# A long-convolution block and its MLP on one core: taps laid apart, evictions in runs of eight, boundary rows shifted by a product, one load queue with six transfers under way

## The chip, the cores and the metric

The kernel runs on one core of a Trainium2 chip. Its time is the device time of one execution in microseconds (us). Five engines work side by side, each through its own list of instructions in order: PE (TensorE, matrix products), DVE (VectorE), ACT (ScalarE), POOL (GpSimd) and SP (SyncE, which here only issues DMA transfers). An instruction that must wait holds up everything behind it in its engine's list.

## The reference

With S = 2048 rows (time), D = 640 channels and F = 1728, all float32:

```python
mod = silu(c) @ w_mod                       # six rows of D: sa, ca, ga, sb, cb, gb
h  = layernorm(x) * (1 + ca) + sa           # x is A_q
ks = sum_t shift(k, t) * shift_k[:, t]      # causal conv of 4 taps along S, per channel
kv = ks * v
y  = longconv(kv, ssm_k) + kv * ssm_D       # causal, length S, per channel (by FFT)
x  = x + ga * (h * y)
h  = layernorm(x) * (1 + cb) + sb
x  = x + gb * (relu(h @ w1 + b1)**2 @ w2 + b2)
```

## The kernel before, in words

**Two stages.** The first computes the long convolution by a transform of length 4096 written as matrix products, in five blocks of 128 channels (`b` = 0 to 4). The second is the MLP over eight chunks of 256 rows with split-precision weights; it is nearly all PE work and the change does not touch it. The second can begin when the last block of the first is done.

**The first stage, per block.** `load_kv(s, u)` brings k and v for a group `s` (group 0 is block 0, groups 1 and 2 are two blocks each) in units `u`: two units for group 0, four for the others, ten in all. A unit is 128 x 1024 numbers; partition p = 32a + n holds, for channel group a, the 64 time steps of segment n. Each unit's k and v come in four transfers of 32 partitions each (128 KB), into two slots for k and two for v in the tile `KV`. `kv(s, u)` forms the 4-tap convolution: four products of k with a tap (one straight into the two-bank PSUM tile `ps6`, three into tiles `up`), three sums into `ps6`, and a product with v into `px[b]` (tiles `S0p`, `S1p`). For groups 0 and 1 two of the four products run on POOL, for group 2 all on DVE. The taps stand in `tapb` (part of `KV`) as they come from memory, channel by channel with the four taps of a channel side by side, so that one tap is read with a step of four numbers.

The first three rows of a unit's k belong to the unit before it (ACT copies them), or, for unit 0, to the neighbouring partition: there POOL clears the three rows and ACT's queue loads them from memory in eight small transfers per group.

`unit_a(b, i, n)` transforms `px[b]` (i = 0) or the filter `ph[b]` (i = 1, loaded by `load_h`) by 64-wide products into two PSUM banks; ACT evicts each bank into the tile `a` with its axes permuted. `spectra` are the second transform, `front` multiplies the two spectra on DVE and POOL, `back` and `unit_y` transform back, `prep` and `finish` apply the layer norm of x and the gate. Beside all this run the six rows of `mod` (loads `wm`) and the row statistics of x (`q_stats`: loads of q, BN_STATS on DVE).

**What sets the order.** The program is recorded as a graph; a planner lists the nodes with costs per engine and with priorities from the table `URGE`, and each engine's list is written out in the planned order. At run time every list is obeyed as it stands. `sp_issue` adds one more rule: each transfer of SP's queue waits until the one `OUT` places ahead of it has landed. All instructions of the graph carry the line number of the call in `emit` (L402), so they are told apart by tiles.

Of the kernel before, what the change touches and what calls it, by code (L numbers as in the profile page):

```python
# [25 lines left out]
OUT = 4  # L26
# [87 lines left out]
class Graph:  # L114
# [101 lines left out]
    def order(self, lag=0.06, pelag=0.1, phase=0.0):  # L216
# [92 lines left out]
        dma_free, landed = 0.0, []  # L309
# [95 lines left out]
def _constants():  # L405
# [17 lines left out]
    for mm in range(1, 32):  # L423
# [32 lines left out]
        "cw": np.hstack([cw, gb[:, 0, 1, 0], gx]).astype(f),  # L456
# [7 lines left out]
def ssm_mlp_kernel(  # L464
# [37 lines left out]
    ident = sb.tile([P, P], F32, tag="ident", name="ident")  # L502
# [7 lines left out]
    cst = sb.tile([P, 256], F32, tag="cst", name="cst")  # L510
# [3 lines left out]
    ca = cst[:, 192:256]  # L514
    warm = sb.tile([P, 1], F32, tag="warm", name="warm")
    nc.scalar.dma_start(cst[:, 0:192], cw_d[:, 0:192])
# [123 lines left out]
    def cost(engine, op, args, kw):  # L640
# [7 lines left out]
        if engine == "DVE":  # L648
            if op == "bn_stats":
                return 0.15 + 0.001 * n  # L650
            if op in ("tensor_mul", "tensor_add", "tensor_sub") and not deep:
                return 0.1 + 0.00115 * n
            if op == "bn_aggr":
                return 0.21
            return 0.17 + 0.001 * n if op != "scalar_tensor_tensor" else 0.17 + 0.00112 * n
# [168 lines left out]
    def load_gi(i):  # L824
        g.key = ("lgi", 0)
        o = slice(8 * i, 8 * i + 8)
        sp_dma(gi[:, 0, o], gi_d.rearrange("p (g c n) -> p g c n", g=16, c=2)[:, o], 4096)
        g.key = ("gi", 0)
        act.activation(gi[:, 1, o, 0], gi[:, 0, o, 1], AF.Copy, scale=-1.0)
        act.activation(gi[:, 1, o, 1], gi[:, 0, o, 0], AF.Copy)  # L830
        if i == 0:
            g.key = ("lgi", 0)
            sp_dma(gi[0:64, 1, 0].rearrange("p c n -> p (c n)"), cw_d[0:64, 192:320], 512)
# [6 lines left out]
    def load_taps(first):  # L840
        g.key = ("ltap", 0)
        if first:
            src = shift_k[:P].rearrange("(a c) t -> a (c t)", a=4)
            sp_dma(tapb[:, 0:128], src.unsqueeze(1).to_broadcast([4, 32, 128]), 512)
            return
        for s in range(2):
            src = shift_k[P + 256 * s : P + 256 * s + 256].rearrange("(a c) t -> a (c t)", a=4)
            sp_dma(tapb[:, 128 + 256 * s : 384 + 256 * s], src.unsqueeze(1).to_broadcast([4, 32, 256]), 1024)
# [4 lines left out]
    def load_kv(s, u):  # L853
# [20 lines left out]
    def kv(s, u):  # L874
# [3 lines left out]
        taps = tapb[:, at : at + 4 * w].rearrange("p (c t) -> p t c", t=4)  # L878
# [3 lines left out]
        for t in range(4):  # L882
            o = sbuf(f"ktmp_{s}_{u}_{t}", (P, n, w), TMP) if t else acc
# [22 lines left out]
    def unit_a(b, i, n):  # L906
# [139 lines left out]
    def load_xp(s, j):  # L1046
# [211 lines left out]
    def mlp_out(n):  # L1258
# [18 lines left out]
        if n < NC - 1:  # L1277
# [4 lines left out]
        ("b1", 0): [-1209, -1601],  # L1282
        ("comb", 0): [-569, -607, -593, -579, -617, -600, -611, -573, -586, -662, -650, -689, -696, -758, -751, -815,
            -822, -847, -840],
        ("comb", 1): [-1052, -1072, -1065, -1058, -1090, -1076, -1083, -1150, -1130, -1136, -1143, -1179, -1186,
            -1213, -1220, -1256, -1263, -1283, -1290],
        ("comb", 2): [-1544, -1493, -1547, -1504, -1554, -1580, -1523, -1573, -1566, -1669, -1662, -1648, -1655,
            -1759, -1720, -1843, -1850, -1864, -1857],
        ("comb", 3): [-2037, -2022, -2047, -2040, -2061, -2065, -2054, -2107, -2100, -2133, -2126, -2140, -2147,
            -2188, -2181, -2214, -2268, -2247, -2261],  # L1290
        ("comb", 4): [-2398, -2412, -2416, -2423, -2429, -2448, -2441, -2456, -2462, -2469, -2505, -2539, -2532,
# [400 lines left out]
```

## Time and profile before

| | us |
|---|---|
| median of 3 runs | 739.98 (738.59 to 777.24) |
| the profiled execution, its own time | 739.45 |
| its span, first to last instruction | 737.7 |
| PE busy | 646.3 (88% of the span) |
| DVE busy | 452.9 (61%) |
| ACT busy | 337.4 (46%) |
| POOL busy | 268.7 (36%) |

The span is what the views divide; 1.75 us of the execution's time lie around it. Busy shares are averages over both stages, which have different limits, so they have to be read stage by stage. A row of a tile view reads: engine, operation, out<-in, count, then the shortest, median and longest duration in ns.

### The profile page before, as it was taken

How to read it: one execution, taken by the hardware profiler on the slowest of the kernel's cores; microseconds unless marked ns; L12 is line 12 of the kernel's file. 1: busy time of each engine (PE TensorE's matmuls, PEld its weight loads, DVE VectorE, ACT ScalarE, POOL GpSimd, SP SyncE). 2: the span in 40 equal slices, each digit the busy share in tenths (PEclk: the TensorE clock that was granted, in tenths of full speed). 3: DMA queues.
4: the chain of work that ended last, by engine and by line, in shares of the span. 5: the costliest groups of instructions: out<-in, count | busy, mean ns of one | idle time of the engine just before them, and what ended most of it. 6: DMA issues, size and time to landing. Idle time of an engine off the chain costs nothing.

```text
span 737.7 us, 17486 instructions
## 1 busy us (share of the span) xinstructions
PE 646.3 (88%) x7401; PEld 574.6 (78%) x7401; DVE 452.9 (61%) x754; ACT 337.4 (46%) x639; POOL 268.7 (36%) x259
## 2 busy tenths in 40 slices
PE   0048798978698989989999999999999999999996
PEld 0047575867577878849999988999999999999896
DVE  1798789789997736786526437446456365464432
ACT  1157256588768798655423424324324233243220
POOL 4647470666655765843311132102103004021001
PEclk9989999988889999998999999999999999999999
DMA  8698689979607521344201011002010020020011
GB/s 113 121 180 194 160 226 234 240 176 190 151 2 150 166 85 45 111 129 129 68 1 42 32 36 36 1 1 72 1 41 33 1 72 1 1 72 1 1 37 36
DMA packets 108155, 62.47 MB, mean 85 GB/s; under 512 B 78316, under 2 KB 98220, under 8 KB 108076
## 3 DMA queue, kind: packets, MB, share of 16 engines
q1 hardware_dynamic: 101884, 58.02, 33.3%
q10 hardware_dynamic: 5936, 3.32, 2.0%
q8 instruction: 58, 0.95, 0.6%
q14 instruction: 21, 0.17, 0.1%
q0 software_dynamic: 256, 0.00, 0.0%
HBM read 52.15 MB, written 9.18 MB: 83 GB/s over the span
## 4 chain that ended last, share of the span: by engine, by line
PE 74%; DVE 7%; DMA 7%; ACT 6%; issue 3%; POOL 3%; SPq 0%; ACTq 0%; DVEq 0%; POOLq 0%
PE ps L402 74%; ACT a L402 5%; DMA KV<-in_A_k_dram 2%; DVE up L402 2%; DMA KV<-in_A_v_dram 2%; DVE ps L402 1%; POOL up L402 1%; DVE wx L402 1%; DMA wm<-in_w_mod_dram 1%; DVE mtmp L402 1%; DMA gb<-in_gb_dram 1%; DMA S1p<-in_A_ssm_k_dram 1%; POOL wx L402 0%; SPq L617 0%; ACTq L402 0%
## 5 line engine op out<-in xcount | busy, mean ns | idle before, releaser
L402 PE MATMUL ps<-xt,w_S 128*128 128x256 f32 (+1 forms) x680 | 129.3, 331 | 0.0
L402 PEld LDWEIGHTS ps<-xt,w_S 128*128 128x128 f32 x680 | 104.8, 190 | 10.3 <-DVE xfs L402 0.2
L402 ACT ACTIVATE mtmp<-ps,b1t 128x256 f32<-128x256 f32 (+1 forms) x112 | 51.4, 473 | 113.7 <-PE ps L402 108.2
L402 PE MATMUL ps<-a,gb 128*64 128x128 f32 x1260 | 82.0, 281 | 8.7 <-DVE wx L402 5.1
L402 PEld LDWEIGHTS ps<-a,gb 128*64 128x64 f32 x1260 | 71.5, 140 | 22.5 <-DVE wx L402 7.4
L402 ACT ACTIVATE a<-ps 128x512 f32<-128x512 f32 x80 | 77.3, 1105 | 20.0 <-PE ps L402 19.7
L402 DVE TENSOR_TENSOR mtmp<-ps,mtmp 128x256 f32<-128x256 f32 (+1 forms) x99 | 41.1, 419 | 69.0 <-ACT mtmp L402 68.0
L402 PE MATMUL ps<-w_S,hring 128*128 128x320 f32 x456 | 78.0, 310 | 0.0
L402 POOL TENSOR_TENSOR wx<-wx 128x256 f32<-128x256 f32 x80 | 68.1, 872 | 20.0 <-DVE wx L402 19.7
L402 PEld LDWEIGHTS ps<-w_S,hring 128*128 128x128 f32 x456 | 70.1, 188 | 1.4
L402 DVE TENSOR_TENSOR hring<-mtmp,hring 128x256 fp32r<-128x256 f32 x74 | 36.3, 496 | 53.8 <-ACT hring L402 53.8
L402 PE MATMUL ps<-cst,S0p 64*64 64x64 f32 x1024 | 24.6, 255 | 50.3 <-DMA KV<-in_A_k_dram 43.2
L402 PEld LDWEIGHTS ps<-cst,S0p 64*64 64x64 f32 x1024 | 21.9, 165 | 55.4 <-DVE S0p L402 45.7
L402 ACT ACTIVATE hring<-mtmp 128x256 fp32r<-128x256 f32 x74 | 30.6, 416 | 67.9 <-PE ps L402 51.3
L402 POOL TENSOR_TENSOR x<-x,gb2row 128x640 f32<-128x640 f32 x16 | 25.3, 1594 | 90.6 <-ACT mtmp L402 90.6
L402 DVE TENSOR_TENSOR wx<-ps,wx 128x512 f32<-128x512 f32 x64 | 40.9, 685 | 22.8 <-PE ps L402 21.8
L402 POOL TENSOR_TENSOR x<-mtmp,x 128x640 f32<-128x640 f32 (+1 forms) x9 | 13.5, 1506 | 108.0 <-DVE mtmp L402 108.0
L402 POOL TENSOR_TENSOR up<-KV 128x1024 f32<-128x1024 f32 x12 | 38.0, 3188 | 27.7 <-DVE ps L402 16.6
L402 DVE TENSOR_TENSOR up<-KV 128x1024 f32<-128x1024 f32 x18 | 43.0, 2396 | 5.3 <-DMA KV<-in_A_k_dram 4.8
L402 DVE SCALAR_TENSOR_TENSOR mtmp<-mtmp 128x256 f32<-128x256 f32 x91 | 44.9, 500 | 1.8
L402 PE MATMUL ps<-gi,wx 64*128 64x128 f32 x640 | 41.5, 278 | 4.4 <-ACT q L402 2.0
L402 ACT ACTIVATE wx<-ps 128x512 f32<-128x512 f32 x49 | 29.5, 608 | 32.3 <-PE ps L402 29.1
(156 smaller groups left out, 1318.6 us busy)
## 6 DMA issues: line engine op xcount, KB each, us to landing
wm<-in_w_mod_dram SPq DMA_DIRECT2D x25, 320.0 KB, 4.1
KV<-in_A_k_dram SPq DMA_DIRECT2D x40, 128.0 KB, 3.7
KV<-in_A_v_dram SPq DMA_DIRECT2D x40, 128.0 KB, 4.5
S1p<-in_A_ssm_k_dram SPq DMA_DIRECT2D x20, 256.0 KB, 5.3
q<-in_A_q_dram SPq DMA_DIRECT2D x8, 640.0 KB, 4.3
out_dram<-x SPq DMA_DIRECT2D x14, 320.0 KB, 3.6
w1s<-in_B_w_dram SPq DMA_DIRECT2D x13, 320.0 KB, 3.4
w2s<-in_B_w_dram SPq DMA_DIRECT2D x13, 320.0 KB, 2.9
```

The source lines that it names most:

```text
L402: fn(*real, **{k: a.real() if isinstance(a, View) else a for k, a in kw.items()})
```

## The change

It does six things:

1. `load_taps` loads the taps into a staging tile and lets ACT copy them into `tapb` tap by tap, so that a product of k with a tap reads neighbouring numbers. Three ACT copies are new.
2. The evictions of `unit_a` walk the bank in another order: they write runs of eight neighbouring numbers where they wrote pairs 32 numbers apart, and read PSUM with a step of 64 numbers.
3. The three boundary rows of each group's unit 0 come as four transfers of 32 partitions into `XP1c`, one product with a shifted identity (`step`) moves them one partition down, and ACT writes them into the k tile, scaled by 0 for the first partition of each channel group and by 1 elsewhere (`later`). POOL's clearing and the 24 small transfers of ACT's queue go.
4. The loads of x for `prep` that ACT issued go to SP's queue.
5. `OUT` is 6 instead of 4.
6. The planner's costs are altered and the table `URGE` is new, so all lists are new.

```diff
-OUT = 4
+OUT = 6
...
-        dma_free, landed = 0.0, []
+        dma_free, landed = 2.5, []
...
-    ident = sb.tile([P, P], F32, tag="ident", name="ident")
+    step = sb.tile([P, P + 1], F32, tag="ident", name="step")
+    ident, step = step[:, 1:], step[:, 0:P]
+    nc.vector.memset(step[:, 0:1], 0.0)
...
+    later = cst[:, 192:193]
...
         if engine == "DVE":
+            if o.buf.name[:3] == "px_":
+                return 0.2 + 0.0017 * n
...
     def load_taps(first):
-        if first:
-            src = shift_k[:P].rearrange("(a c) t -> a (c t)", a=4)
-            sp_dma(tapb[:, 0:128], src.unsqueeze(1).to_broadcast([4, 32, 128]), 512)
-            return
-        for s in range(2):
...
+        raw = sbuf(f"tap_{int(first)}", (P, D), [whole(f"STG{i}") for i in range(4)])
+        for s in (0,) if first else (1, 2):
+            at, w = (0, 128, 384)[s], WIDE[s]
...
+            copy(
+                act,
+                tapb[:, at : at + 4 * w].rearrange("p (t c) -> p c t", t=4),
+                raw[:, at : at + 4 * w].rearrange("p (c t) -> p c t", t=4),
+            )
...
         if u == 0:
-            pool.memset(kt[:, 0:3], 0.0)
-        else:
-            copy(act, kt[:, 0:3], KT[s, u - 1][:, n : n + 3])
+            end = sbuf(f"kend_{s}", (P, 3, w), [part(parent("XP1", 2560), 2048, ("XP1c",))])
         for a in (0, 2, 1, 3):
...
             if u == 0:
-                act_dma(kt[32 * a + 1 : 32 * a + 17, 0:3], kshift[0:16, 0:3, cols], 4 * w)
-                act_dma(kt[32 * a + 17 : 32 * a + 32, 0:3], kshift[16:31, 0:3, cols], 4 * w)
+                sp_dma(end[32 * a : 32 * a + 32], ksrc[:, 61:64, cols], 4 * w)
...
+        if u == 0:
+            t = psum(f"kend_{s}", (P, 3, w), ANY)
+            with g.as_one(0.3):
+                mm(t.rearrange("p i c -> p (i c)"), step, end.rearrange("p i c -> p (i c)"), True, True)
+            act.activation(kt[:, 0:3], t, AF.Copy, scale=later)
+        else:
+            copy(act, kt[:, 0:3], KT[s, u - 1][:, n : n + 3])
...
-        taps = tapb[:, at : at + 4 * w].rearrange("p (c t) -> p t c", t=4)
+        taps = tapb[:, at : at + 4 * w].rearrange("p (t c) -> p t c", t=4)
...
-            o = AX[b][i].rearrange("p m (e d g) -> p m g e d", e=2, d=2)[:, :, 8 * n : 8 * n + 8, e]
-            copy(act, o, t[e].rearrange("p g m d -> p m g d"))
+            o = AX[b][i].rearrange("p m (e d g) -> p m e d g", e=2, d=2)[:, :, e, :, 8 * n : 8 * n + 8]
+            copy(act, o, t[e].rearrange("p g m d -> p m d g"))
...
-            (act_dma if h else sp_dma)(
-                t[64 * h : 64 * h + 64], qsrc[h, :, 4 * j : 4 * j + 4, BASE[s] : BASE[s] + w], 4 * w
-            )
+            sp_dma(t[64 * h : 64 * h + 64], qsrc[h, :, 4 * j : 4 * j + 4, BASE[s] : BASE[s] + w], 4 * w)
...
-        ("kv", 0): [-140, -127, -153, -153, -178, -202, -227, -239, -255, -267, -280, -226, -292, -177, -304, -316],
...
+        ("pa", 0): [-279, -289, -259, -269, -299, -308, -313, -318, -422, -427, -441, -446, -479, -484, -469, -474],
```

**Place 1: the start of SP's list** (transfers; `gb` is a constant of the second transform, `S1p` the filter of block 0, `XP1p` the staged boundary rows, `tap` the staged taps). Before:

```order
L617 DMA KV<-in_A_shift_k_dram 128x1x256
L617 DMA KV<-in_A_k_dram 32x32x32 x2
L617 DMA KV<-in_A_shift_k_dram 128x1x256
L617 DMA KV<-in_A_v_dram 32x32x32 x2
L617 DMA KV<-in_A_shift_k_dram 128x1x128
L617 DMA KV<-in_A_k_dram 32x32x32 x4
L617 DMA KV<-in_A_v_dram 32x32x32
```

The same place in the changed list:

```order
L621 DMA gb<-in_gb_dram 128x1024
L621 DMA KV<-in_A_k_dram 32x32x32 x3
L621 DMA XP1p<-in_A_k_dram 32x3x32
L621 DMA KV<-in_A_k_dram 32x32x32 x2
L621 DMA XP1p<-in_A_k_dram 32x3x32
L621 DMA KV<-in_A_k_dram 32x32x32 x2
L621 DMA tap_122<-in_A_shift_k_dram 128x1x128
L621 DMA KV<-in_A_v_dram 32x32x32
L621 DMA XP1p<-in_A_k_dram 32x3x32
L621 DMA KV<-in_A_k_dram 32x32x32
L621 DMA S1p<-in_A_ssm_k_dram 32x32x64
```

The constant `gb` and the filter of block 0 have moved ahead of most of v; the four filter transfers end at the 24th transfer of the list (they ended at the 34th), and the last quarter of v for unit 1 of group 0 stands 38th, behind the first two loads of q (it stood 21st).

**Place 2: the start of DVE's list** (`ps` the sum in PSUM, `up` a product, `S0p` the result for block 0; `s<-q` and `st<-s` are statistics of x). Before:

```order
L402 TENSOR_TENSOR up_132<-KV 128x1024
L402 TENSOR_TENSOR ps_96<-KV 128x1024
L402 TENSOR_TENSOR ps_96<-ps_96,up_132 128x1024 x3
L402 TENSOR_TENSOR S0p<-ps_96,KV 128x32x32
L402 TENSOR_TENSOR ps_96<-KV 128x1024
L402 TENSOR_TENSOR up_132<-KV 128x1024
L402 TENSOR_TENSOR ps_96<-ps_96,up_132 128x1024
```

The same place in the changed list:

```order
L402 TENSOR_TENSOR ps_97<-KV 128x1024
L402 TENSOR_TENSOR up_142<-KV 128x1024
L402 TENSOR_TENSOR ps_97<-ps_97,up_142 128x1024 x3
L402 TENSOR_TENSOR S0p<-ps_97,KV 128x32x32
L402 BN_STATS s_200<-q_148 128x6
L402 TENSOR_TENSOR up_142<-KV 128x1024
L402 TENSOR_TENSOR ps_97<-KV 128x1024
L402 TENSOR_TENSOR ps_97<-ps_97,up_142 128x1024
L402 BN_STATS s_200<-q_148 128x6
```

Statistics of x now stand between the two units of group 0 (eight BN_STATS and four BN_AGGR of the first two q tiles before the second `S0p`), where there were none before the third unit was done.

**Place 3: ACT's list up to the first evictions** (`a0` is the transform of `px`, `a1` that of the filter). Before:

```order
L402 ACTIVATE KV_87<-KV_87 128x96
L402 ACTIVATE gb_134<-gb_134 64x1024 x2
L402 ACTIVATE gi_144<-gi_144 128x8x64 x2
L402 DMA KV_87<-in_A_k_dram 15x3x64 x2
L402 DMA KV_87<-in_A_k_dram 16x3x64
L402 DMA KV_87<-in_A_k_dram 15x3x64
L402 DMA KV_87<-in_A_k_dram 16x3x64 x3
L402 DMA KV_87<-in_A_k_dram 15x3x64
L402 ACTIVATE KV_87<-KV_87 128x192
L402 ACTIVATE gb_134<-gb_134 64x1024 x2
L402 ACTIVATE a0_0_186<-ps5_95 128x32x8x2
```

The same place in the changed list:

```order
L402 ACTIVATE gb_101<-gb_101 64x1024 x2
L402 ACTIVATE KV_88<-tap_1_122 128x32x4
L402 ACTIVATE KV_88<-KV_88 128x96
L402 ACTIVATE KV_88<-ps0_91,cst_75 128x96
L402 ACTIVATE KV_88<-tap_0_137 128x64x4 x2
L402 ACTIVATE a1_0_165<-ps3_94 128x32x2x8
```

No transfer of k is left in ACT's list, and the filter of block 0 is transformed and evicted first (`a1`), with the transform of `px` (`a0`) after it; PE's list has the same exchange.

More of the change, by code (lines that the diff above doesn't have):

```diff
@@ L832, in load_gi @@
             g.key = ("lgi", 0)
[L833 removed]
+            sp_dma(gi[0:64, 1, 0].rearrange("p c n -> p (c n)"), cw_d[0:64, 193:321], 512)
     px, ph, KT, VT = {}, {}, {}, {}
@@ L882, in kv @@
         for t in range(4):
-            o = sbuf(f"ktmp_{s}_{u}_{t}", (P, n, w), TMP) if t else acc
+            o = sbuf(f"ktmp_{s}_{u}_{t}", (P, n, w), TMP, line="ktmp") if t else acc
             own = t > 1 and s in KP
@@ new lines, in ssm_mlp_kernel @@
+        ("gate", 0): [-1901, -1911, -1941, -1921, -1931, -2604, -2649, -2654, -2679, -2684, -2705, -2718, -2633,
+            -2638, -2643, -2690, -2725, -2736, -2745],
+        ("gb", 0): [-152, -163, -380, -370],
+        ("gi", 0): [-358, -352, -714, -720],
+        ("h", 1): [-825, -858, -889, -900, -1072, -1087, -1094, -1107, -1155, -1165, -1173, -1188, -1210, -1224,
+            -1228, -1238],
+        ("h", 2): [-1422, -1451, -1440, -1457, -1530, -1641, -1548, -1599, -1635, -1647, -1663, -1678, -1717, -1737,
+            -1755, -1775],
@@ new lines, in ssm_mlp_kernel @@
+        ("h", 3): [-1862, -1887, -1871, -1893, -2052, -2071, -2070, -2087, -2108, -2121, -2117, -2127, -2164, -2173,
+            -2178, -2189],
+        ("h", 4): [-2369, -2387, -2389, -2412, -2416, -2437, -2438, -2453, -2470, -2485, -2492, -2508, -2520, -2531,
+            -2557, -2572],
+        ("hat", 0): [-2838, -2827],
+        ("hat", 1): [-2855, -2870],
[7 rows of a table added]
+        ("lgb", 0): [-17, -327],
+        ("lgi", 0): [-302, -594, -657],
[23 rows of a table added]
+        ("ltap", 0): [-106, -175, -197, -282, -202, -286],
[18 rows of a table added]
@@ new lines, in ssm_mlp_kernel @@
+        ("out", 0): [-3563, -3508, -3594, -3517, -3519, -3550, -3837, -3849],
+        ("pa", 0): [-279, -289, -259, -269, -299, -308, -313, -318, -422, -427, -441, -446, -479, -484, -469, -474],
+        ("pa", 1): [-704, -709, -686, -691, -727, -732, -800, -799, -955, -960, -965, -990, -985, -1005, -1015,
+            -1025],
+        ("pa", 2): [-1247, -1274, -1295, -1300, -1304, -1309, -1252, -1257, -1379, -1389, -1403, -1413, -1363, -1369,
+            -1453, -1458],
+        ("pa", 3): [-1782, -1787, -1772, -1777, -1822, -1827, -1805, -1810, -1904, -1909, -1900, -1933, -1938, -1966,
+            -1980, -1995],
@@ new lines, in ssm_mlp_kernel @@
+        ("pra", 2): [-1520, -1557, -1505, -1530, -1566, -1539, -1636, -1622, -1704, -1694, -1715, -1720, -1743,
+            -1748, -1758, -1753],
+        ("pra", 3): [-2051, -2046, -2077, -2082, -2153, -2138, -2277, -2148, -2203, -2259, -2208, -2184, -2475,
+            -2480, -2471, -2466],
+        ("pra", 4): [-2056, -2061, -2066, -2101, -2133, -2158, -2162, -2143, -2282, -2180, -2248, -2213, -2514,
+            -2547, -2537, -2542],
+        ("prm", 0): [-1354, -1324, -1417, -1441],
+        ("prm", 1): [-1530, -1603, -1641, -1880],
@@ new lines, in ssm_mlp_kernel @@
+        ("prm", 2): [-1596, -1721, -1887, -1894],
+        ("prm", 3): [-2114, -2339, -2311, -2486],
+        ("prm", 4): [-2107, -2188, -2346, -2552],
+        ("prp", 0): [-1368, -1341, -1451, -1484],
+        ("prp", 1): [-1577, -1614, -1668, -1901],
+        ("prp", 2): [-1648, -1846, -1915, -1987],
+        ("prp", 3): [-2175, -2353, -2327, -2527],
+        ("prp", 4): [-2156, -2209, -2366, -2566],
+        ("qp", 0): [-655, -746, -766, -845],
+        ("qp", 1): [-1131, -1190, -1467, -1510],
```

151 lines of the change are left out of this document (59 added, 92 removed), and 309 rows, old and new, of the table URGE.

## The prediction

> **What bounds the kernel now.** I first cut the span into stages: from the start to PE's first product, to the end of group 1's convolution, to the end of group 2's, to the MLP, and the MLP (columns: stretch, its length, busy time and instructions of PE, PE's weight loads, DVE, ACT, POOL, then granted clock, DMA share, GB/s).
>
> ```profile
> 0.00:43.25 43.25, 0.00 (x1) 0.00 (x1) 21.95 (x16) 6.88 (x10) 21.37 (x24) 1.00 0.80 130
> 43.25:113.40 70.15, 56.90 (x1228) 47.94 (x1228) 59.22 (x65) 36.81 (x50) 40.34 (x30) 0.93 0.83 191
> 113.40:226.00 112.60, 94.68 (x1864) 76.83 (x1865) 101.65 (x123) 82.08 (x140) 62.02 (x61) 0.91 0.72 161
> 226.00:331.00 105.00, 97.33 (x1751) 76.36 (x1751) 69.46 (x105) 79.04 (x139) 67.14 (x67) 1.00 0.42 115
> 331.00:737.70 406.70, 397.42 (x2562) 373.50 (x2562) 200.57 (x449) 132.61 (x301) 77.81 (x80) 0.99 0.12 33
> ```
>
> From 331 us PE is busy 397 of 407 us, and from 226 us 97 of 105: nothing here shortens that work. Whatever is won is won before 226 us, where PE does 151.6 us of work and so has 74 us of slack; it works there at a granted clock of 0.93 and 0.91. Some start-up stays, so the floor is far below anything I forecast.
>
> Next the chain of waits, and who holds PE before 226 us.
>
> ```profile
> PE ps L402 74%; ACT a L402 5%; DMA KV<-in_A_k_dram 2%; DVE up L402 2%; DMA KV<-in_A_v_dram 2%; DVE ps L402 1%; POOL up L402 1%; DVE wx L402 1%; DMA wm<-in_w_mod_dram 1%; DVE mtmp L402 1%; DMA gb<-in_gb_dram 1%; DMA S1p<-in_A_ssm_k_dram 1%; POOL wx L402 0%; SPq L617 0%; ACTq L402 0%
> ...
> 168.33 3.82 ACT a L402 x4
> ...
> 266.06 3.22 ACT a L402 x4
> ```
>
> The largest item after PE is the eviction `a`, in runs of several: there PE waits for banks. But the engine that runs through from 17 to 226 us is DVE, with the convolution of k. Its units end here (the last product of a unit writes `S0p`):
>
> ```profile
> 16.65 1.97 DVE L402 TENSOR_TENSOR up<-KV 128x1024 f32<-128x1024 f32 x1 [4.82 <-DMA KV<-in_A_k_dram]
> ...
> 41.25 1.95 DVE L402 TENSOR_TENSOR S0p<-ps,KV 128x1024 f32<-128x1024 f32 x1
> ...
> 43.25 4.68 PEld L402 LDWEIGHTS ps<-cst,S0p 64*64 64x64 f32 x192 [43.25 <-DVE S0p L402]
> ...
> 112.29 1.92 DVE L402 TENSOR_TENSOR S0p<-ps,KV 128x512 f32<-128x512 f32 x2 [2.06 <-DMA KV<-in_A_v_dram]
> ...
> 224.81 1.05 DVE L402 TENSOR_TENSOR S0p<-ps,KV 128x512 f32<-128x512 f32 x1
> ```
>
> DVE is busy 59.2 + 101.7 = 160.9 of the 182.8 us between 43.25 and 226 (88%), and 21.95 us of the 26.6 ahead of it. PE gets the last blocks only at 226. So the forecast is DVE's sum over this stretch, with DMA and PE as the limits that could take its place.
>
> **The change, part by part.**
>
> *Taps.* The products of k with a tap, beside rows of like size without the step:
>
> ```profile
> L402 DVE TENSOR_TENSOR up<-KV x18: 1962/2106/3393, 16.6 to 219.1; 128x1024 f32<-128x1024 f32 x18
> L402 DVE TENSOR_TENSOR ps<-KV x10: 1926/2066/4755, 18.5 to 211.9; 128x1024 f32<-128x1024 f32 x10
> L402 DVE TENSOR_TENSOR up<-KV 128x1024 f32<-128x1024 f32 x18 | 43.0, 2396 | 5.3 <-DMA KV<-in_A_k_dram 4.8
> L402 DVE TENSOR_TENSOR ps<-KV 128x1024 f32<-128x1024 f32 x10 | 27.3, 2728 | 0.1
> ...
> L402 DVE TENSOR_TENSOR ps<-ps,up x30: 1215/1232/1233, 23.2 to 221.3; 128x1024 f32<-128x1024 f32 x30
> L402 DVE TENSOR_TENSOR up<-up,row x20: 675/692/1772, 163.6 to 298.3; 128x512 f32<-128x512 f32 x20
> L402 POOL TENSOR_TENSOR up<-KV x12: 2848/2884/4692, 16.7 to 102.6; 128x1024 f32<-128x1024 f32 x12
> L402 POOL TENSOR_TENSOR up<-up,row x20: 1269/1277/3132, 165.0 to 300.3; 128x512 f32<-128x512 f32 x20
> ```
>
> Undisturbed, a product takes about 1.95 us; an unstepped sum of the same size takes 1.23, and the product with a row in runs of 32 takes 0.69 for half the size, so about 1.3 for the whole. That is 0.65 to 0.72 us less for each of 28. But the means are 2.40 and 2.73: some 0.55 us more, in instructions that lie beside POOL's, and that part need not shrink. Bounds: 28 x 0.65 = 18 us if the disturbance stays whole, and (43.0 + 27.3) - 28 x 1.3 = 34 us if it goes. I take a mean of 1.6 us (it stays for the most part, over shorter instructions): 70.3 - 44.8 = **25.5 us off DVE**, all before 226 us. POOL's 12 products go from 2.88 to about 2 x 1.28 = 2.56 us, 4 us in all, beside DVE.
>
> The row of 1.95 against 1.23 has its rule in the Trainium skill, "Vector Engine (DVE) Microarchitecture Reference", section 5.2, where a source that hops at every element costs 1.73 ns per column and a contiguous one 1.054; the trace agrees in direction, though its stepped products are slower (1.95 us for 1024). By the page's figures alone the saving would be an estimate of 28 x 0.69 = 19 us, and the forecast below some 6 us later.
>
> The three copies that turn the taps (128, 256 and 256 numbers) have no row; the nearest are
>
> ```profile
> L402 ACT ACTIVATE a<-ps x80: 1034/1108/1194, 48.2 to 281.1; 128x512 f32<-128x512 f32 x80
> L402 ACT ACTIVATE q<-ps x39: 576/597/658, 99.5 to 313.2; 128x512 f32<-128x512 f32 x39
> ```
>
> so 0.2 to 0.7 us each; I take 0.4. The first stands ahead of DVE's first product but waits for less data than k does, and ACT is idle then (6.9 of 43.25 us busy): nothing. Without that cover it costs 0.4 us.
>
> *Evictions.* `q<-ps` has the shape that the new `a<-ps` gets: PSUM read with a step of 64, runs of eight written. So 1.11 becomes 0.60 us, for 80 evictions 41 us off ACT. Bounds: 0.58 (q's shortest) to 1.11, no gain. On the path is only where PE waits for banks: the two pieces quoted halve, about 1.9 and 1.6 us. The first lies before 226 us, where DVE sets the end, so I count it nothing; of the second I take 1.5 us, and another 1.5 for the like pieces behind 226, out of 105.0 - 97.3 = 7.7 us of idle PE: **3 us**. ACT is then off the path everywhere.
>
> *Boundary rows and one queue.* ACT loses 24 issues. SP gains 12 small transfers and the loads of x:
>
> ```profile
> L617 SPq DMA_DIRECT2D KV<-in_A_k_dram x40: 311/327/1558, 1.6 to 188.6; - x40
> L402 ACTq DMA_DIRECT2D KV<-in_A_k_dram x24: 322/420/1488, 6.2 to 91.6; - x24
> ...
> SPq L617 <- PE ps L402: 29.9, 8, 25.0
> SPq L617 <- DMA KV<-in_A_k_dram: 29.5, 29, 5.6
> ...
> KV<-in_A_k_dram SPq DMA_DIRECT2D x40, 128.0 KB, 3.7
> KV<-in_A_v_dram SPq DMA_DIRECT2D x40, 128.0 KB, 4.5
> ```
>
> (The last two rows give the median us from issue to landing.) 24 more issues at 0.33 us are 8 us of SP, over 226 us in which SP mostly waits: nothing, as long as waiting covers them, and 8 us if not. The product and its ACT write are new in three places. Ahead of DVE's second product in group 0 they cost PE and ACT about a microsecond where ACT before copied rows and waited for small transfers; for groups 1 and 2 PE's list holds the product between other work, and if its rows are late, PE stands. I bound the three by nothing and by one landing each, 3 x 3.7 us, and take nothing, because PE waits there for DVE anyway.
>
> *Six under way and the new order at the start.* Beside a DMA share of 0.80 in the first 43.25 us, SP's waits for transfers just landing say that four in flight did not fill the engines. In the new list the last quarter of v for unit 1 lies behind 7.0 MB (shapes summed). At the old rate (5.6 MB by 43.25 us, then 191 GB/s) it lands at 50.6 us; at 130 / 0.80 = 162 GB/s at 43. I take 46, **3 us later** than 43.25 for the second `S0p`. Against this, DVE has by then done eight statistics, and PE the whole transform of the filter:
>
> ```profile
> L402 DVE BATCH_NORM_STATS2 s<-q x32: 440/476/503, 69.5 to 148.4; 128x6 f32<-128x320 f32 x32
> ...
> 81.23 3.62 PE L402 MATMUL ps<-cst,S1p 64*64 64x64 f32 x128 [3.12 <-POOL S1p L402]
> 65.43 6.96 PE L402 MATMUL ps<-a,gb 128*64 128x128 f32 x121
> ```
>
> That is 8 x 0.48 = 4 us of DVE's sum in a time when it waits for v, and on PE up to 2 x 3.62 + 6.96 = 14 us (256 products of the filter's first transform and most of its second stand ahead of `S0p`; I count 10, since the rows hold some slow clock).
>
> *The sum.* DVE had 21.95 + 59.22 + 101.65 = 183 us of work from 16.65 to 226 and so 26.5 us idle. With 25.5 us less work and its gaps at 26.5 + 6 = 32.5 us (3 for the later v; 3 because a faster DVE waits more often for PE and loads; the 4 us of statistics only fill a gap) the last `S0p` comes 25.5 - 6 = 19.5 us earlier, near 206. PE must then fit its 151.6 us, less what the better clock gives, between 46 and 206 with 10 us done before: 142 of 160 us, 89%, against 83% before. It fits, tightly. With the 3 us behind it the gain is 22.5 us; from the profiled execution's 739.45 us that gives **717**. This execution lies 0.5 us under the median of the runs.
>
> **Rivals.**
> - *The loads set the pace* (726 us). If six in flight bring no more than four, group 1 still ends near 112, as the 2.06 us wait for v at 112.29 hints. Then only group 2's 16 products count: 16 x 0.9 = 14 us, less 3.5 of new waits, plus 3: 13.5. For it: shares of 0.80 and 0.83. Against: SP's waits are for single landings.
> - *Products stay disturbed* (726). The saving is 18 us, gaps grow by 7.5, plus 3: 13.5. The Trainium skill, "SBUF — State Buffer", Terms, says DVE and GpSimd hold their shared ports exclusively for a whole instruction; the long maxima (4.76 beside 1.93) agree.
> - *Everything lines up* (704). The saving is 34 us, the gaps do not grow, the tail gives 3, less 1.5 for PE's crowding: 35.5.
> - *The evictions do not shrink* since each read now hops in PSUM: the change doesn't do what it says. The 3 us go, and PE's tight stretch loses about 4 more: 724. The row of q speaks against it.
> - *Slower: the refill of the k and v slots.* Landing takes 3.7 us for k and 4.5 for v with four under way. If the engines are already full, six stretch this by half, 1.9 and 2.3 us, and small transfers stand between. A unit's slot is refilled while DVE works on the other slot; from the point where refilling takes longer than that unit's work, each of eight units adds up to 4.2 us: 34 us. 739.45 - 22.5 + 34 = 751.
>
> **How the numbers follow.** The forecast, 710 to 724, has 0.50; loads 0.14; disturbed products 0.13; all lined up 0.12; evictions 0.05; slower 0.06. The range of 703 to 731 leaves out the slower case and the ends of the others. A change of 2% (14.8 us) is about what can be told from none: faster than 725 takes the forecast, the lined-up case, evictions and part of the two at 726, 0.70; within 2% 0.25; slower by more 0.05 (the far half of the last rival and what I have not seen).
>
> **What would show it.** `up<-KV` and `ps<-KV` near 1.3 us shortest, 1.6 mean; `a<-ps` near 0.60; first evictions of the filter before 35 us (its loads end after 3.5 MB, 27 us at 130 GB/s); the second `S0p` at 43 to 50; the last near 206; the stage after it still about 102 us; the MLP's 407 us unchanged. The forecast is wrong if the products keep 1.9 us, if DVE's gaps before the last `S0p` pass 45 us, or if the MLP's part moves.

## The result, and the profile after

| | before | changed |
|---|---|---|
| median, us | 739.87 (4 runs, 738.59 to 777.24) | 723.02 (4 runs, three of them 721.23 to 723.57) |
| profiled execution, own time | 739.45 | 723.57 |
| its span | 737.7 | 721.8 |

The changed kernel takes 0.977 of the time before, 95% interval 0.974 to 0.980, some 17 us less. The comparison leaves out the longest run of each kernel, which lies far from its others (777 and 2677 us). Forecast were 717 and a range of 703 to 731.

The span of the changed kernel in stretches (columns as in the prediction): from DVE's first product of k to the last `S1p`, which closes the convolution, on to the last sum `up` ahead of the MLP, on to PE's first product with `xt`, and the MLP.

```profile
16.40:205.98 189.58, 151.34 (x3094) 124.09 (x3095) 155.29 (x202) 99.99 (x200) 103.37 (x92) 0.93 0.86 177
205.98:303.27 97.29, 94.46 (x1742) 75.26 (x1738) 62.74 (x97) 67.91 (x134) 66.97 (x66) 1.00 0.47 133
303.27:316.19 12.92, 3.04 (x13) 2.09 (x13) 12.74 (x13) 5.78 (x11) 8.42 (x5) 0.63 0.63 183
316.19:721.80 405.61, 396.52 (x2565) 372.82 (x2565) 197.69 (x441) 128.62 (x296) 74.98 (x77) 0.99 0.10 28
```

The kernel before, cut at the same events:

```profile
16.65:226.78 210.13, 152.36 (x3140) 125.55 (x3144) 183.34 (x200) 123.27 (x197) 118.23 (x96) 0.93 0.77 169
226.78:322.83 96.05, 91.59 (x1692) 73.16 (x1685) 60.78 (x92) 75.75 (x131) 62.18 (x62) 1.00 0.41 114
322.83:329.55 6.72, 4.09 (x18) 1.75 (x18) 6.45 (x13) 2.33 (x6) 2.88 (x3) 1.00 0.46 156
329.55:737.70 408.15, 398.30 (x2567) 374.17 (x2567) 202.02 (x450) 132.85 (x303) 79.27 (x81) 0.99 0.11 32
```

The convolution ends 20.8 us earlier (226.78 to 205.98). The stretch behind it is 1.2 us longer, and the short one ahead of the MLP, in which PE has 3 us of work, grows from 6.72 to 12.92 us: 7.4 us are given back there. The MLP is 2.5 us shorter. 20.8 - 7.4 + 2.5 = 15.9 us, the difference of the two spans. (Before, PE made a few first products and waited again until 331.22 us; counted from there, the short stretch grows by 4.5 us and the MLP is only 0.9 us shorter.)

The groups that the change was to shorten (busy us, mean ns, idle time ahead):

```profile
L402 DVE TENSOR_TENSOR up<-KV 128x1024 f32<-128x1024 f32 x18 | 25.2, 1406 | 5.5 <-ACT KV L402 5.3
L402 DVE TENSOR_TENSOR ps<-KV 128x1024 f32<-128x1024 f32 x10 | 13.3, 1328 | 7.7 <-DMA KV<-in_A_k_dram 7.7
...
L402 ACT ACTIVATE a<-ps 128x512 f32<-128x512 f32 x80 | 42.7, 597 | 28.8 <-PE ps L402 28.6
```

and, with shortest, median and longest duration in ns, and the second `S0p`:

```profile
L402 DVE TENSOR_TENSOR up<-KV x18: 1172/1244/2569, 19.6 to 200.0; 128x1024 f32<-128x1024 f32 x18
L402 POOL TENSOR_TENSOR up<-KV x12: 2334/2367/3405, 19.6 to 100.7; 128x1024 f32<-128x1024 f32 x12
```
```profile
42.63 1.96 DVE L402 TENSOR_TENSOR S0p<-ps,KV 128x1024 f32<-128x1024 f32 x1 [1.60 <-DMA KV<-in_A_v_dram]
```

The products of k fall from 70.3 to 38.5 us and the evictions from 77.3 to 42.7. Whether these two, or the order and the queue, moved the end of the convolution cannot be read from one trace. The experiments tell.

### The profile page after: what moved, and what is told of

Read it like the earlier page. It is cut to its first block, busy times and chain, and to the rows that moved or that the text cites. A ratio compares the mean times of both kernels' runs of the same rounds, so it can differ in the third digit from the quotient of the medians.

```text
span 721.8 us, 17456 instructions
## 1 busy us (share of the span) xinstructions
PE 645.4 (89%) x7407; PEld 574.3 (80%) x7407; DVE 428.7 (59%) x755; ACT 307.9 (43%) x645; POOL 259.7 (36%) x256
## 4 chain that ended last, share of the span: by engine, by line
PE 80%; DVE 8%; DMA 4%; issue 3%; ACT 2%; SPq 1%; POOL 0%; DVEq 0%; POOLq 0%; ACTq 0%
PE ps L402 80%; DVE up L402 2%; SPq L621 1%; DMA S1p<-in_A_ssm_k_dram 1%; DVE mtmp L402 1%; DMA XP0p<-in_A_q_dram 1%; DVE wx L402 1%; DVE w_S L402 1%; DMA KV<-in_A_k_dram 1%; DVE ps L402 1%; ACT a L402 1%; DMA x<-x_d 1%; DMA XP1p<-in_A_k_dram 1%; ACT up L402 1%; DVE x L402 1%
## 5 line engine op out<-in xcount | busy, mean ns | idle before, releaser
L402 PE MATMUL ps<-a,gb 128*64 128x128 f32 x1260 | 85.0, 286 | 10.8 <-DVE wx L402 4.7
L402 PEld LDWEIGHTS ps<-a,gb 128*64 128x64 f32 x1260 | 73.9, 143 | 22.5 <-issue 9.9
L402 DVE TENSOR_TENSOR mtmp<-ps,mtmp 128x256 f32<-128x256 f32 (+1 forms) x99 | 41.0, 420 | 71.2 <-ACT mtmp L402 70.3
L402 DVE TENSOR_TENSOR hring<-mtmp,hring 128x256 fp32r<-128x256 f32 x74 | 39.9, 548 | 64.5 <-ACT hring L402 64.4
L402 POOL TENSOR_TENSOR wx<-wx 128x256 f32<-128x256 f32 x80 | 65.3, 835 | 28.8 <-DVE wx L402 26.1
L402 POOL TENSOR_TENSOR x<-mtmp,x 128x640 f32<-128x640 f32 (+1 forms) x9 | 13.1, 1465 | 123.9 <-DVE mtmp L402 123.9
L402 ACT ACTIVATE a<-ps 128x512 f32<-128x512 f32 x80 | 42.7, 597 | 28.8 <-PE ps L402 28.6
L402 PE MATMUL ps<-cst,S1p 64*64 64x64 f32 x1536 | 30.4, 232 | 17.6 <-POOL S1p L402 10.4
L402 PE MATMUL ps<-xt,w_S1a 128*128 128x256 f32 (+1 forms) x170 | 37.9, 342 | 7.6 <-DVE xfs L402 6.0
L402 PEld LDWEIGHTS ps<-cst,S1p 64*64 64x64 f32 x1536 | 27.5, 145 | 20.6 <-POOL S1p L402 10.6
L402 POOL TENSOR_TENSOR mtmp<-mtmp 128x256 f32<-128x256 f32 (+1 forms) x21 | 15.0, 723 | 79.7 <-ACT mtmp L402 79.5
L402 PEld LDWEIGHTS ps<-gi,wx 64*128 64x128 f32 x640 | 38.7, 193 | 4.9 <-issue 4.2
```

Source lines behind the costliest of these rows:

```text
L402: fn(*real, **{k: a.real() if isinstance(a, View) else a for k, a in kw.items()})
```

## The experiments

Times are compared by their ratio to the kernel before, which ran on the same chip beside them; 0.1% is 0.74 us. What is read inside a kernel is from one profiled execution each, and such readings scatter: the changed kernel and those of experiments 9 to 11, whose lists are the same up to there, end the convolution between 203.9 and 206.0 us, so a difference of 2 us in that place says nothing.

**1. Taps read in steps again, all else as changed.**

```diff
-  tapb[:, at : at + 4 * w].rearrange("p (t c) -> p c t", t=4),
-  raw[:, at : at + 4 * w].rearrange("p (c t) -> p c t", t=4),
+  tapb[:, at : at + 4 * w],
+  raw[:, at : at + 4 * w],
...
-  taps = tapb[:, at : at + 4 * w].rearrange("p (t c) -> p t c", t=4)
+  taps = tapb[:, at : at + 4 * w].rearrange("p (c t) -> p t c", t=4)
```

> The changed kernel with its taps read in steps of four again (the three copies stay, but move the numbers unturned); order, queue and evictions as in the changed kernel. If DVE's sum sets the end of the convolution, the 28 products of k go back to means near 2.4 and 2.7 us (now 1.41 and 1.33), DVE has about 32 us more, the last S0p falls at 232 to 238 us instead of 206, and the whole takes 748 to 756 us, more than the kernel before. If the new order and the six transfers had brought the gain and the taps lay beside waits, the whole stays under 735 us.

Measured: 727.47 us, ratio 0.9824 (0.978 to 0.987). The products went back to long durations, and the end hardly moved:

```profile
L402 DVE TENSOR_TENSOR up<-KV 128x1024 f32<-128x1024 f32 x18 | 40.9, 2278 | 2.5 <-ACT KV L402 2.3
L402 DVE TENSOR_TENSOR ps<-KV 128x1024 f32<-128x1024 f32 x10 | 23.5, 2345 | 7.5 <-DMA KV<-in_A_k_dram 7.4
```
```profile
15.90:208.85 192.95, 152.72 (x3116) 124.25 (x3116) 180.48 (x202) 101.12 (x203) 119.88 (x92) 0.94 0.86 175
```

DVE has 25.9 us more of these products; the last `S1p` ends at 208.85, 2.9 us later (this execution, 723.99 us, is the fastest of the four). DVE's idle time fell from some 34 to 12.5 us (192.95 - 180.48) and took the rest. So in the new order DVE's sum does not set the end of the convolution. The theory behind the forecast missed here by more than 20 us, and the rival (the order brought it, the taps lie beside waits) held, so far.

**2. Evictions in pairs again, all else as changed.**

```diff
-  o = AX[b][i].rearrange("p m (e d g) -> p m e d g", e=2, d=2)[:, :, e, :, 8 * n : 8 * n + 8]
-  copy(act, o, t[e].rearrange("p g m d -> p m d g"))
+  o = AX[b][i].rearrange("p m (e d g) -> p m g e d", e=2, d=2)[:, :, 8 * n : 8 * n + 8, e]
+  copy(act, o, t[e].rearrange("p g m d -> p m g d"))
```

> The changed kernel with the evictions of the first stage written in pairs again; order unchanged. The evictions go back to 1.11 us (now 0.60), 41 us more on ACT. By the prediction's term this costs 3 us, all behind the last S0p: 726.5 us. If the tight part ahead of it counts too (PE has 150.6 us of work in 186 us there), it costs 8 us or more: 731 us or above. If ACT is off the path everywhere, nothing: 723 to 724 us.

Measured: 728.71 us, ratio 0.9864 (0.981 to 0.992), 0.9% or 7 us above the changed kernel, between the first case and the second; the interval leaves room for both. The profiled executions are 5.3 us apart. The last `S1p` comes 1.2 us later (207.15), no more than the scatter, and the stretch from there to the first product of `xt` is 4.1 us longer (114.3 against 110.2). So in the new order most of the cost lies behind the convolution, where the first case had it, and not in the tight part ahead of it.

**3. Four transfers under way at run time, order as changed.**

```diff
-        if len(queued) > OUT:
+        if len(queued) > 4:
...
-  tc.add_manual_dep(nc.cur_bb.bb.instructions[-1], queued[-1 - OUT], info, reason="place in time")
+  tc.add_manual_dep(nc.cur_bb.bb.instructions[-1], queued[-1 - 4], info, reason="place in time")
```

> The changed kernel with four transfers under way at run time instead of six; instructions and their order unchanged. If the engines are filled by four as well, nothing changes: 722 to 725 us. If six are what brought group 1's end forward, the loads of k and v come later: the first end of a unit some 3 us, the last S0p 5 to 10 us, the whole 728 to 734 us.

Measured: 728.85 us, ratio 0.9848 (0.981 to 0.988), 6 us above the changed kernel: the second case. The last `S1p` ends at 211.76. Up to there, the chain of waits by line, and the length, busy times and DMA share:

```profile
by line: DMA KV<-in_A_v_dram 22.7%; DMA S1p<-in_A_ssm_k_dram 12.8%; PE ps L402 12.2%; DMA wm<-in_w_mod_dram 11.6%; DMA KV<-in_A_k_dram 10.4%; DMA q<-in_A_q_dram 7.1%; DMA XP0p<-in_A_q_dram 3.8%; DVE up L402 3.4%; SPq L621 3.1%; DMA gi<-in_g
```
```profile
15.90:211.76 195.86, 151.63 (x3092) 123.19 (x3094) 162.70 (x202) 100.27 (x200) 103.65 (x92) 0.92 0.77 172
```

With four, transfers hold the path and fill 0.77 of the engines; with six they fill 0.86 and PE holds 61.8% of the path.

**4. Eight transfers under way** (the same edit with 8).

> The changed kernel with eight transfers under way at run time instead of six; instructions and their order unchanged. Four instead of six cost about 6 us. If the loads still set the end of the convolution, eight bring the last S0p to 200 to 203 us and the whole 3 to 6 us less. If the engines are full at six, the whole stays within 2 us of the changed kernel; if single landings grow longer, 1 to 3 us more.

Measured: 722.31 us, ratio 0.9783 (0.975 to 0.982), the same as with six; the last `S1p` ends at 205.58. Landing times (median us in the last column), with four and with eight:

```profile
KV<-in_A_k_dram SPq DMA_DIRECT2D x40, 128.0 KB, 3.6
KV<-in_A_v_dram SPq DMA_DIRECT2D x40, 128.0 KB, 3.3
```
```profile
KV<-in_A_k_dram SPq DMA_DIRECT2D x40, 128.0 KB, 5.4
KV<-in_A_v_dram SPq DMA_DIRECT2D x40, 128.0 KB, 5.5
```

With six, the landings are at 5.1 and 5.2 us and the share of the engines is 0.86; with eight the share is 0.86 too, and each transfer only takes a little longer.

**5. and 6. The kernel before with the taps alone, and with the evictions alone.** For the taps, one line (the copies that turn them are left out, here and in experiment 7, so a column meets other taps than its own):

```diff
-  taps = tapb[:, at : at + 4 * w].rearrange("p (c t) -> p t c", t=4)
+  taps = tapb[:, at : at + 4 * w].rearrange("p (t c) -> p t c", t=4)
```

For the evictions, the two lines of experiment 2 the other way round.

> The kernel before, with only the products of k reading their taps in runs of 32 or 64 instead of steps of four (the numbers are not turned, so each column is multiplied by other taps than its own); order, queue and evictions as before. Taken back alone from the changed kernel, the same edit cost only about 4 us, because DVE had 32 us of idle time there. If DVE's sum is the limit of the old order, as the prediction had it, the last S0p comes 18 us or more earlier and the whole takes 714 to 723 us. If PE and the loads stand close behind DVE in the old order too, the whole takes 728 to 736 us. If taps gain nothing without the new order, 737 to 741 us.

> The kernel before, with only the evictions of the first stage written in runs of eight; order, queue and taps as before. By the prediction's term 3 us, all behind the last S0p: 736 to 737 us. If they are worth as much as in the new order, where going back to pairs cost about 6 us, 733 to 734 us. If DVE alone sets the old order's end, 739 us.

Measured: taps alone 732.18 us, ratio 0.9931 (0.990 to 0.996); evictions alone 735.48 us, ratio 0.9982 (0.996 to 1.000). The taps gave 0.7%, the second case; the evictions 0.2%, if anything, between the first case and the last. The profiled execution of the evictions alone (737.36 us) is among the slowest of its ten, at a granted clock of 0.90 ahead of the last `S1p` (0.93 in the kernel before), so what is read from it below may be some 2 us late.

**7. The kernel before with both.**

> The kernel before with both edits of layout, the taps in runs (numbers not turned, so that columns meet other taps than their own) and the evictions in runs of eight; order and queue as before. Alone they gave about 5 us and 1 us. If the two add up, 6 to 7 us less than before (ratio about 0.991). If each opens what the other closes, as with the new order, 9 to 12 us less (ratio 0.984 to 0.988). In neither case the 17 us of the whole change, if the order is a third part without which DVE stands waiting: its idle time ahead of the last S0p, 39.7 us with the taps alone, stays above 35 us.

Measured: 720.56 us, ratio 0.9765 (0.973 to 0.980). The two layout edits, in the old order and with four transfers under way, bring all that the whole change brings. None of the three cases foretold it: alone 5.1 and 1.3 us, together 17. My expectation that the order is a needed third part was wrong. The chain of waits by line and PE's waits for evictions, from 16.65 us to the last `S1p`, tell why. Taps alone:

```profile
by line: PE ps L402 35.2%; ACT a L402 17.1%; DMA KV<-in_A_k_dram 7.5%; DMA wm<-in_w_mod_dram 6.3%; issue 6.1%; DMA KV<-in_A_v_dram 4.5%; POOL up L402 3.5%; DVE ps L402 3.4%; DMA gb<-in_gb_dram 3.0%; DVE wx L402 2.9%; DVE up L402 1.9%; ACT u
```
```profile
PE ps L402 <- ACT a L402: 11.5, 9, 3.9
```

Taps and evictions:

```profile
by line: PE ps L402 48.3%; DMA KV<-in_A_k_dram 9.6%; DMA KV<-in_A_v_dram 6.0%; issue 5.6%; DMA wm<-in_w_mod_dram 5.2%; DVE ps L402 3.6%; POOL up L402 3.6%; DVE up L402 3.5%; DMA S1p<-in_A_ssm_k_dram 2.9%; DMA XP0p<-in_A_q_dram 2.6%; DVE wx 
```
```profile
PE ps L402 <- ACT a L402: 4.8, 4, 2.8
```

With the taps apart but the evictions long, the evictions hold 17.1% of the path (13.1% in the kernel before): DVE is done sooner and then waits. Its idle time rises from 26.8 to 39.7 us. Its waits for PE are no longer than with both edits (15.1 and 16.0 us). The wait that goes with the short evictions is one for ACT, whose list holds the normalized pieces of x (`up`) between the evictions; with the taps alone:

```profile
DVE up L402 <- ACT up L402: 5.4, 2, 3.9
```

With both edits it is 0.8 us, and the kernel before has none. With the taps alone ACT works from 157 to 178 us without a pause, much of it on evictions, and DVE waits 3.9 us at the end of that. So the second chain beside DVE's is ACT's list, for which PE and DVE both wait. With short evictions but stepped taps, DVE's sum of 183.2 us holds the end (227.1). Only with both does the end come forward as far as 212.43. Of the 10.4 us between the profiled executions with the taps alone and with both, 6.6 lie ahead of the last `S1p`, 1.6 behind it, and 2.2 in the MLP, which neither edit touches: over its first 70 us the granted clock was 0.95 with the taps alone, as before, and 1.00 with both. Whether the edits brought that clock is not shown.

**8. Taps and evictions both taken back, order and queue as changed** (the edits of 1 and 2 together).

> The changed kernel with both taps (read in steps of four) and evictions (in pairs) taken back; the new order, one queue, six under way and the product for the boundary rows stay. If the two costs add up (4 and 6 us), the whole takes 732 to 734 us, and order and queue are worth 6 to 7 us by themselves. If each edit had only hidden behind the other, so that DVE and ACT now both hold PE, 738 us or more. If they share one slack, 728 to 730 us.

Measured: 734.08 us, ratio 0.9951 (0.992 to 0.998). Alone the two cost 0.5% and 0.9%, together 1.8%: between the first case and the second. What is left for order, queue and boundary rows is 0.5%, 3.6 us. All eight combinations, with the profiled times (idle time and waits up to the last `S1p`, from 16.65 us in the old order and 15.9 in the new):

| order and queue | taps | evictions | ratio | last `S1p` ends | from there to `xt` | DVE idle ahead | PE's waits for evictions |
|---|---|---|---|---|---|---|---|
| old | steps | pairs | 1 | 226.8 | 102.8 | 26.8 | 10.4 |
| old | runs | pairs | 0.993 | 219.0 | 103.6 | 39.7 | 11.5 |
| old | steps | eights | 0.998 | 227.1 | 101.4 | 27.3 | 3.2 |
| old | runs | eights | 0.977 | 212.4 | 102.0 | 33.5 | 4.8 |
| new | steps | pairs | 0.995 | 212.3 | 114.1 | 16.4 | 13.5 |
| new | runs | pairs | 0.986 | 207.2 | 114.3 | 34.4 | 13.1 |
| new | steps | eights | 0.982 | 208.9 | 107.8 | 12.5 | 7.9 |
| new | runs | eights | 0.977 | 206.0 | 110.2 | 34.8 | 5.7 |

Down the sixth column, the new order gives back 6 to 11 us behind the convolution beside every combination of the edits; beside both edits it wins 6.4 us ahead of it (212.4 to 206.0) and loses 8.2 behind it (102.0 to 110.2).

**9. Where it is given back.** The chain of waits of the changed kernel from the last sum to `xt` (start, us, what):

```profile
303.27 0.69 DVE up L402
...
304.07 1.26 DVE nm L402
...
305.42 0.61 DVE mtmp L402
306.03 2.34 DVE w_S L402 x2
308.38 0.40 issue
308.78 0.53 DVE xfs L402
309.31 2.81 DVE w_S L402 x2
312.11 3.36 DVE xt L402 x2
```

Four subtractions of weights for later blocks of the MLP stand on DVE ahead of and between the steps that make `xt`. The experiment puts them behind, by a dependence in the plan:

```diff
+    final = max(n.id for n in g.nodes if n.key == ("xt", 0))
+    for n in g.nodes:
+        if n.key in (("wl", 7), ("wl", 8)):
+            n.deps.add(final)
```

> The changed kernel with four subtractions of weights (w_S of blocks 7 and 8 of both matrices) held on DVE until the five pieces of xt are written; the plan behind this point is drawn up anew. In the changed kernel 12.9 us pass from the last sum up to the first product of the MLP (8.4 us before), and DVE spends 5.2 us of them on these four subtractions. If they are what was given back, the stretch shrinks to 6.5 to 8.5 us and the whole takes 717 to 719 us. If the statistics, the transposes or a shared port set this stretch, or if the delayed subtractions hold PE later, the whole stays at 722 to 725 us.

(The 8.4 us count to the long run of products; to the first product with `xt` it is 6.72.) Measured: 719.40 us, ratio 0.9716 (0.968 to 0.975); its four runs, 717.2 to 719.9, all lie below those of the changed kernel. The stretch shrank from 12.92 to 8.70 us (301.01 to 309.71). Time and stretch lie just above the bounds of the first case. The 4.2 us are not the whole account: in this execution the convolution also ended 1.8 us earlier, within the scatter, and the MLP took 2.0 us longer (407.6). This is the fastest kernel of the case that computes everything. DVE there:

```profile
305.36 0.55 DVE L402 TENSOR_SCALAR xfs<-ps,cbs 128x256 f32<-128x256 f32 x1 [1.59 <-PE ps L402]
307.51 3.23 DVE L402 TENSOR_TENSOR xt<-xfs,xt 128x256 fp32r<-128x256 f32 x2 [1.60 <-ACT xt L402]
...
311.24 0.99 DVE L402 TENSOR_TENSOR xt<-xfs,xt 128x256 fp32r<-128x256 f32 x2
```

The first pair of subtractions takes 3.23 us, the second 0.99, and POOL works through four additions to x beside the first.

**10. and 11. POOL's additions moved.** First by the same kind of dependence, in the plan:

```diff
+        late = n.engine == "POOL" and n.key == ("f2", 0)
+        if late or n.key in (("wl", 7), ("wl", 8)):
```

> The changed kernel with the four subtractions of weights held until xt is written, and POOL's four additions of the bias row to x held until then too. With the subtractions alone held, the first two subtractions for xt still took 3.23 us beside POOL's additions (0.43 us each elsewhere). If POOL is what lengthens them, they take about 0.9 us, and the whole comes to 716 to 717.5 us (719.4 with the subtractions alone). If it is the kind of output, they keep 3.2 us and the whole stays at 719 to 720 us.

Measured: 724.66 us, ratio 0.9836 (0.980 to 0.987): slower, and no test of the question. The edit caught two of the four, and a dependence in the plan is no wait at run time: POOL ran the others in their place, and the first pair still took 2.10 us, the second 2.88. Then with the plan of 9 and a real wait:

```diff
+    late = [x for x in plan[:at] if x[2].engine == "POOL" and x[2].key[0] == "f2"]
+    g.emit([x for x in plan[: at + 1] if x not in late])
...
+        tc.add_manual_dep(nc.cur_bb.bb.instructions[-1], xt_end, info, reason="behind xt")
```

> The changed kernel with the four subtractions of weights held behind xt, as before, and with POOL's four additions to x really held: they wait for the last subtraction of xt. (In the run before, only two of them were moved, and only in the plan; POOL ran the other two at once.) If POOL's additions are what lengthens the first two subtractions of xt from 0.9 to 3.2 us, these take 0.9 to 1.3 us, the stretch from the last sum up to the first product of the MLP shrinks from 8.7 to about 6.4 us, and the whole takes 0.3% less than with the subtractions alone (about 717 us beside 739.7 for the kernel before). If not, the ratio stays at 0.972 to 0.974.

Measured: 721.64 us, ratio 0.9777 (0.975 to 0.981). DVE:

```profile
308.53 0.76 DVE L402 TENSOR_TENSOR xt<-xfs,xt 128x256 fp32r<-128x256 f32 x2 [1.19 <-ACT xt L402]
...
312.21 2.92 DVE L402 TENSOR_TENSOR w_S<-w2s,w_S 128x640 fp32r<-128x640 f32 x2
315.05 4.30 DVE L402 TENSOR_TENSOR w_S<-w1s,w_S 128x640 fp32r<-128x640 f32 x2
```

and POOL:

```profile
312.37 6.29 POOL L402 TENSOR_TENSOR x<-x,gb2row 128x640 f32<-128x640 f32 x3 [8.87 <-DVE xt L402]
```

The pair takes 0.76 us with POOL still, 3.23 with POOL beside it: that POOL's additions lengthen it is shown. The time is nevertheless worse. The stretch was only 0.6 us shorter (8.13 us), and the additions now meet the four subtractions of weights, which take 7.2 us (3.6 in experiment 9), and the later pieces of `xt`; from the first product on, the kernel takes 410.8 us instead of 407.6.

**12. Less work for PE.** Accumulating products get fewer columns:

```diff
+LIGHT = {("mr", 0): 64, ("mr", 1): 64, ("mr", 2): 64, ("qp", 0): 32, ("qp", 1): 32, ("qp", 2): 32}
...
+                if op == "matmul" and not kw["start"] and n.key in LIGHT:
+                    cut = LIGHT[n.key]
+                    real[0], real[2] = real[0][:, 0:cut], real[2][:, 0:cut]
```

> The changed kernel with less work for PE ahead of the last S0p, in the same order: the accumulating products of the modulation rows (48 of 0.50 us) are cut from 320 columns to 64, and those of the inverse transform of blocks 0 to 2 (96 of 0.29 us) from 128 to 32; the rest of those sums is left out. PE's busy time up to 206 us falls from 151 to some 120 to 130 us. If PE and what hangs on it now set the end of the convolution, the last S0p falls at 185 to 198 us. If the loads or DVE set it, it stays at 202 to 207 us. The total says little here, since work is left out behind 206 us as well.

Measured: 720.90 us, ratio 0.9772 (0.973 to 0.981); the last `S1p` ends at 202.68, 3.3 us earlier than in the changed kernel and 1.2 us below its scatter. It lies within the bounds of the second case, at their edge, but PE's load hardly fell, so the run does not decide between the cases, and what sets the end of the convolution in the new order stays open. Cutting the columns saved little. The changed kernel:

```profile
L402 PE MATMUL ps<-gi,wx 64*128 64x128 f32 x352 | 23.6, 287 | 0.0
L402 PE MATMUL ps<-wm,XP0p 128*128 128x320 f32 x48 | 18.0, 497 | 0.0
```

This run, with the products that were cut and those beside them that were not:

```profile
L406 PE MATMUL ps<-gi,wx 64*128 64x128 f32 x192 | 24.7, 346 | 0.8 <-POOL wx L406 0.8
L406 PE MATMUL ps<-gi,wx 64*128 64x32 f32 x192 | 16.2, 248 | 0.0
L406 PE MATMUL ps<-wm,XP0p 128*128 128x64 f32 x36 | 6.7, 298 | 0.3 <-DMA wm<-in_w_mod_dram 0.3
L406 PE MATMUL ps<-wm,XP0p 128*128 128x320 f32 x12 | 4.7, 519 | 0.4 <-DMA wm<-in_w_mod_dram 0.4
```

## Why the prediction came out, and where its reasons did not

The time and the side of the forecast held; several of its steps did not, and that the total came near is in part luck. Forecast were 19.5 us ahead of the end of the convolution and 3 us behind it; measured are 20.8 ahead, 7.4 lost behind, and 2.5 in the MLP, where nothing was forecast.

- *The products.* Forecast 25.5 us off DVE, measured 31.8 (70.3 to 38.5), because most of what POOL's presence added went too: the means fell to 1.41 and 1.33 us, not 1.6. That part depends on the order. In the old order the same taps in runs took 31.7 + 17.7 = 49.4 us, 20.9 less than before, at means of 1.76 and 1.77, nearer to the forecast's assumption. POOL's own products came to a median of 2.37 us where 2.56 was expected. Undisturbed, a product lost 0.79 us (shortest 1.96 to 1.17); the estimate from the Trainium skill, "Vector Engine (DVE) Microarchitecture Reference", section 5.2, was 0.69.
- *DVE's whole sum and its gaps.* DVE's work from its first product to the last `S1p` is 155.3 us (forecast 183 - 25.5 = 157.5), its gaps there about 34 (32.5), the second `S0p` ends at 44.6 (46), the last `S0p` at 203.8 (206), the last `S1p` at 205.98. The totals agree to some 2 us, but by luck: the products gave 6.3 us more than forecast, and DVE's other work ahead of the last `S1p`, which the sum left as it was, grew by 3.8 us (113.0 to 116.8).
- *That DVE's sum sets the end* is the step that failed. "The engine that runs through from 17 to 226 us is DVE" was true, but it stood beside a second chain, ACT's list with the long evictions, nearly as long. Experiment 5 takes 20.9 us off DVE's products and gets 7.7 us there and 5 in all; experiment 1 puts 25.9 us back and loses 2.9 there. The forecast needed the second chain to go as well, and counted the evictions there as nothing.
- *"The first lies before 226 us, where DVE sets the end, so I count it nothing."* Here it failed in a number. Next to short taps the short evictions bring the end forward by 6.6 us in the old order (219.0 to 212.4), and the time by 12 us, of which some 2 lie in the MLP. The 3 us counted behind 226 are 1.4 to 1.6 in the old order and 4.1 to 6.3 in the new (sixth column). The price of the rival in which they do not shrink, 7 us, came out in number (0.9%), but not in place: it had 3 us behind the convolution and 4 ahead of it, where experiment 2 shows 4.1 behind and 1.2 ahead.
- *The stage behind, "about 102 us".* It took 110.2. Of the 8 us, the four subtractions of weights cost 4.2, as experiment 9 shows (2.0 of them come back in its MLP), in a stretch that the forecast had not looked at; it compared orders only ahead of the last `S0p`. Beside them the pair of subtractions for `xt` lost 2.5 us to POOL's additions.
- *Six under way and the new order.* Forecast as nearly neutral. In the changed kernel six instead of four are worth 6 us, and with four the transfers hold the path; so the condition of the rival "the loads set the pace", that six bring no more than four, did not hold. Yet the old order with four under way and both edits is as fast (0.9765 and 0.977). So order, queue and boundary rows together bring nothing beside the two layout edits, for they spend behind the convolution what they win ahead of it. The boundary rows alone were not tried. They were counted as nothing, but DVE waits for ACT's writes of them ahead of its second product (1.9 us) and in group 1 (3.4 us), a wait that the kernel before does not have:

```profile
DVE up L402 <- ACT KV L402: 5.3, 2, 3.4
```

- *The slower rival*, six transfers stretching the refill: landings did grow (k 3.7 to 5.1 us), but the share rose with them, and eight cost nothing either.
- *The MLP* was to stay, and nearly did: 405.6 against 408.2 us, or 406.5 without the few early products.

Not tried: the old order of the last stretch behind the new order's start, which by the table would put 206.0 and 102 together, some 8 us below the changed kernel, if nothing moves.

## What to carry to other kernels

An engine that is busy 88% of a stretch need not be the only bound of it: before pricing its work at full value, ask which wait ends last when it is done sooner, and test two suspected edits together as well as apart, since 0.7% and 0.2% may make 2.35%. When a new order wins ahead of a hand-over, read the last instructions before the hand-over too: work that could wait, queued in front of it on an in-order engine, gives the gain back. And a dependence that only a planner sees is not a wait on the chip.

## What the runs showed of the hardware

Two subtractions on DVE with both sources in SBUF took 0.76 us with POOL still (experiment 11) and 2.10 to 3.42 us beside its additions (the changed kernel, experiments 9 and 10). The Trainium skill, "SBUF — State Buffer", Terms, says that DVE and GpSimd hold their shared port pair for the whole of an instruction, while the loser waits; these numbers agree, though they do not show the port itself. Moving POOL's additions moved the loss to the next DVE work instead of removing it.

Cutting every second of a row of products from 128 to 32 columns (experiment 12) saved nothing: the cut ones took 248 ns and the whole ones beside them 346, 297 on average, where all whole they had taken 287. Products cut from 320 to 64 columns took 298 ns instead of 497. PE's busy time from 16 to 206 us went from 151.4 to 149.8 us as other work moved up, and its granted clock there was 0.91 instead of 0.93.
